# DeltaNet and FNet mixing on one Trainium2 core: another order of the same pieces of work, with fourteen more groups of unread TensorE products

## The chip, the core and the metric

The kernel runs on one core of a Trainium2 chip. Its engines are TensorE (PE in the profile, with PEld for its weight loads), VectorE (DVE), ScalarE (ACT) and GpSimd (POOL); SyncE (SP) issues most of the transfers. The metric is the device time of one execution in microseconds (us), lower is better. The kernel before takes 620.09 us, the median of three runs (620.94, 620.09 and 619.37).

## What is computed

The first half is a delta rule with a state of 48 by 48 for each of 4 batches and 8 heads; the second half mixes the result with two Fourier transforms and sends it through a small network.

```python
k_n = k / (norm(k) + 1e-06)                    # q, k, v: (4, 8, 768, 48)
for t in range(768):
    y[t] = q[t] @ state                        # 48 x 48 for each batch and head
    state += beta[t] * outer(k_n[t], v[t] - k_n[t] @ state)
x = y reshaped to (4, 768, 384)
u = x + real(fft(fft(x, axis=1), axis=2))
un = (u - mean) / sqrt(var + 1e-06)            # over the 384 columns
out = u + relu(un @ w_ch1) @ w_ch2             # 384 x 1536 and 1536 x 384
```

## The kernel before

**Units.** Tokens are handled 128 at a time: 6 tiles for each of 4 batches make 24 units, and a unit holds all 8 heads. Inside a tile the step-by-step rule becomes matrix products: the keys' products with each other give a triangular matrix for each head, which is inverted; queries, keys and values go through it, and only one state step for each half tile (64 tokens) depends on the one before it. For a unit the pieces are: load of k, q and v by SyncE (line 407); "turn", transposes of k and q on TensorE (`tr`, line 353, eight instructions at a time) with copies out of PSUM to SBUF (`copy`: line 359 on ScalarE, line 361 on VectorE); the keys' products (line 350) and their eviction into `gd` on VectorE (line 546); the inverse on VectorE; the queries' products, evicted by line 573; the state chain; the outputs, which free the unit's slot.

**Rounds.** Units 0 and 1 form the first round, 2 to 5 the second, and then come rounds of 4, 4, 4, 3 and 3 units. In the first two rounds the inverse is built of blocks of 16 (`invert16`): one transpose of 32 by 32 blocks into `rr` (line 689), a few row operations on `nr` and `gb` (lines 694 to 729, of which 729 only readies a factor for the values, used by line 605), then fourteen steps of a product and a sum (lines 749 and 755) for each round, a scaling (768), two transposes (774, 778), and a `join` of blocks on TensorE and VectorE (lines 809 and 855). In later rounds `invert` does it in thirty steps on blocks of 32 (lines 936 and 941). Units wait in slots: six of `us` and two in R1; unit 11 also uses columns of a tile that the row views call `R`.

**The second half.** For each batch: folds of the sequence on VectorE (line 1353), two transforms as products on TensorE, layer norm, and the network's two products (tiles `w` and `R`). Its weights are rounded and split before by ScalarE, VectorE and GpSimd (lines 1955 to 1975; line 1972 is GpSimd's). All of TensorE's products go through one helper, line 350; what a product belongs to is told by its tiles.

**The order.** Nothing is issued when it is written down. `P.op` of the class `Plan` (lines 135 to 181) only records a piece: what it issues, and which engines may do it. There are 2882 pieces. The text ORDER (lines 57 to 132) then names them in the order of issue, two signs for each; after the number stands a sign for the engine where a piece has a choice (ScalarE or VectorE for most copies out of PSUM; GpSimd or VectorE for the zeroing of padding, `pads`, line 487), a sign for each of the 8 PSUM banks that it takes, and for a load that SyncE issues the piece after which it may start. `issue` (lines 153 to 179) decodes it. Each engine works through its own instructions in that order, and waits where an input or a buffer isn't ready. Between any two engines only these data waits and the paced loads set the timing.

**Unread products.** A number past the last piece calls `fill` (defined at the end of the kernel's function) with a kind and a bank. Kind 4 is one product of a constant, `pack`, 128x128 by 128x256, into a PSUM bank (line 2178); kind 3 is the same in two products of 64 rows; kind 0 is 18 products of 64x64 (line 2172), issued once at the very start. Nothing reads them. A matmul of 32-bit numbers appears twice in the trace, so that the trace counts two for each product that the program issues.

## Time and profile before

| | before |
|---|---|
| median of three runs | 620.09 us |
| the profiled execution's own time | 620.75 us |
| its span in the trace | 618.9 us |
| mean granted TensorE clock | 0.997 |
| busy: PE, DVE, ACT, POOL | 600.3, 538.4, 272.4, 29.6 us |
| records of the trace: PE, DVE, ACT, POOL | 9742, 1500, 758, 39 |
| DMA, mean over the span | 52 GB/s |

The span is what the trace covers; the execution's own time is 1.85 us longer, and that rest is taken as the same for both kernels. Busy time is the sum of what an engine's instructions took. A row of the timeline has its start and its length in us, the engine, the kernel's line, the output and inputs by the program's names, the shapes and a count; in brackets stands the time for which the engine was idle before it, and what ended that wait. A row of the windows gives, for a stretch of the span, the busy time and count of instructions of each engine, the clock that TensorE was granted, and the DMA engines' busy share.

### The profile page before, as it was taken

What the parts mean: (1) busy time and instruction counts of PE and PEld (TensorE: products, weight loads), DVE (VectorE), ACT (ScalarE), POOL (GpSimd) and SP (SyncE); (2) the same over time, 40 slices, a digit from 0 to 9 for tenths busy, and PEclk for the clock granted to TensorE, in tenths of its full rate; (3) what the DMA queues carried; (4) which work ended last, traced back from release to release, by engine and by line L of the source; (5) the groups of instructions that cost most, each with busy time, mean ns of one, the idle gap of its engine ahead of it and who ended that gap; (6) DMA issues with size and microseconds to landing.
All of it is one profiled execution on the core that took longest, in us unless ns stands there. A gap on an engine that the chain in (4) does not pass through costs nothing.

```text
span 618.9 us, 22537 instructions
## 1 busy us (share of the span) xinstructions
PE 600.3 (97%) x9742; PEld 523.0 (85%) x9742; DVE 538.4 (87%) x1500; ACT 272.4 (44%) x758; POOL 29.6 (5%) x39
## 2 busy tenths in 40 slices
PE   8799899999999999999999999999999999999997
PEld 7578889767777777889888878898899899999997
DVE  5989998999898989999889999998996897878655
ACT  5699667552355354634543323444353304222120
POOL 2003410220000000000000000000000000000000
PEclk9899999999999999999999999999999999999999
DMA  8743554521023222020212121000010000000001
GB/s 162 195 134 103 125 144 120 135 64 35 5 42 70 53 58 66 2 40 14 54 29 66 28 52 28 19 21 15 2 41 4 28 1 2 27 1 26 1 2 51
DMA packets 85440, 31.98 MB, mean 52 GB/s; under 512 B 75996, under 2 KB 80829, under 8 KB 85341
## 3 DMA queue, kind: packets, MB, share of 16 engines
q1 hardware_dynamic: 85149, 30.31, 19.9%
q8 instruction: 76, 1.25, 0.8%
q10 hardware_dynamic: 192, 0.23, 0.1%
q14 instruction: 23, 0.19, 0.1%
HBM read 25.82 MB, written 4.72 MB: 49 GB/s over the span
## 4 chain that ended last, share of the span: by engine, by line
PE 83%; DVE 11%; ACT 2%; issue 2%; DMA 1%; POOL 0%; DVEq 0%; POOLq 0%; ACTq 0%
PE pp L350 79%; PE pp L353 3%; DVE R L1353 2%; ACT us L359 1%; PE pp L2178 1%; DVE pm L1353 1%; DMA us<-in_q_dram 1%; DVE eo L1353 1%; PE pp L2172 1%; DVE rr L689 1%; DVE x L1328 0%; DMA R<-in_moe_w_ch_dram 0%; POOL w L1972 0%; DVE gd L546 0%; DVE tmp L749 0%
## 5 line engine op out<-in xcount | busy, mean ns | idle before, releaser
L350 PE MATMUL pp<-R,w 128*128 128x256 f32 (+1 forms) x832 | 180.6, 366 | 0.0
L350 PEld LDWEIGHTS pp<-R,w 128*128 128x128 f32 x832 | 144.9, 190 | 18.6 <-issue 0.4
L350 PE MATMUL pp<-w,R 128*128 128x384 f32 (+1 forms) x288 | 91.0, 440 | 0.1
L350 PE MATMUL pp<-us 64*64 64x64 f32 (+5 forms) x2704 | 87.6, 233 | 2.2 <-ACT us L359 1.0
L359 ACT ACTIVATE us<-pp 128x512 f32<-128x512 f32 (+4 forms) x149 | 58.6, 402 | 60.4 <-PE pp L350 37.7
L350 PEld LDWEIGHTS pp<-us 64*64 64x64 f32 (+3 forms) x2704 | 74.2, 134 | 8.4 <-ACT us L359 2.8
L350 PEld LDWEIGHTS pp<-w,R 128*128 128x128 f32 x288 | 51.7, 190 | 21.7 <-DVE st L1291 0.2
L936 DVE TENSOR_TENSOR tmp<-rr 128x168 f32<-128x168 f32 (+9 forms) x150 | 50.8, 341 | 2.9
L941 DVE TENSOR_TENSOR rr<-rr,tmp 128x168 f32<-128x168 f32 (+10 forms) x150 | 49.4, 331 | 3.2
L350 PEld LDWEIGHTS pp<-u,us 64*64 64x64 f32 (+1 forms) x1360 | 34.1, 130 | 9.1 <-issue 3.9
L350 PE MATMUL pp<-u,us 64*48 64x48 f32 (+2 forms) x1360 | 40.1, 217 | 1.5 <-DVE mv L361 0.6
L359 ACT ACTIVATE R<-pp 128x384 f32<-128x384 f32 (+9 forms) x60 | 24.4, 426 | 27.3 <-PE pp L353 16.5
L1795 DVE TENSOR_TENSOR us<-us,pp 128x256 f32<-128x256 f32 x64 | 25.9, 417 | 11.8 <-ACT us L359 7.2
L1830 ACT ACTIVATE R<-pp 128x512 f32<-128x512 f32 x23 | 13.7, 596 | 45.0 <-PE pp L350 34.8
L359 ACT ACTIVATE u<-pp 64x192 f32<-64x192 f32 (+1 forms) x60 | 19.6, 326 | 26.4 <-DVE x L1899 13.7
L350 PE MATMUL pp<-R,ws 128*128 128x192 f32 x144 | 28.5, 328 | 0.2 <-issue 0.2
L350 PE MATMUL pp<-us,gd 128*128 128x192 f32 x144 | 27.6, 327 | 0.0
L1607 ACT ACTIVATE R<-pp 128x512 f32<-128x512 f32 x22 | 13.0, 595 | 32.3 <-PE pp L350 32.2
L359 ACT ACTIVATE us<-us,nr 128x48 f32<-128x48 f32 x112 | 26.5, 323 | 0.3 <-DMA us<-in_v_dram 0.2
L350 PE MATMUL pp<-st,us 48*64 48x48 f32 (+1 forms) x1104 | 25.0, 222 | 1.2 <-issue 1.1
L1328 DVE TENSOR_TENSOR x<-x,pp 64x192 f32<-64x192 f32 x66 | 23.2, 351 | 2.1 <-PE pp L350 0.9
L350 PEld LDWEIGHTS pp<-ft,R 97*128 97x128 f32 (+1 forms) x192 | 23.0, 191 | 1.8 <-ACT R L359 0.9
(208 smaller groups left out, 1076.2 us busy)
## 6 DMA issues: line engine op xcount, KB each, us to landing
out_dram<-x SPq DMA_DIRECT2D x11, 384.0 KB
us<-in_k_dram SPq DMA_DIRECT2D x16, 192.0 KB
us<-in_q_dram SPq DMA_DIRECT2D x16, 192.0 KB
us<-in_v_dram SPq DMA_DIRECT2D x16, 192.0 KB
x<-in_moe_w_ch_dram SPq DMA_DIRECT2D x11, 242.0 KB
R<-in_moe_w_ch_dram SPq DMA_DIRECT2D x8, 256.0 KB
ws<-in_moe_w_ch_dram SPq DMA_DIRECT2D x5, 242.0 KB
us<-in_k_dram SPq DMA_DIRECT2D x6, 181.5 KB
```

What stands on the lines that cost most here:

```text
L350: I(nc.tensor.matmul(o, lhsT=lhsT, rhs=rhs, start=start, stop=stop, skip_group_check=True))
L353: I(nc.tensor.matmul(o, lhsT=src, rhs=ident[p0:p0 + n, p0:p0 + n], is_transpose=True, start=start, stop=True, skip_group_check=True))
L359: I(nc.scalar.activation(o, i, ACT.Copy, **({} if scale is None else {"scale": scale})))
L689: vec(1760, lambda e: I(nc.vector.transpose(R, ro.gd(0, 4).rearrange("p (n c) -> p c n", c=32))), [ro.agd(0, 4)], [aR], pr)
L936: I(eng(e).tensor_tensor(T_, R[:, :, j + 1:32, j:j + 1].broadcast_to([128, ns, n, j]), R[:, :, j:j + 1, 0:j].broadcast_to([128, ns, n, j]) ...
L941: I(eng(e).tensor_tensor(R[:, :, j + 1:32, 0:j], R[:, :, j + 1:32, 0:j], T_, op=ALU.add))
L1328: I(nc.vector.tensor_tensor(w, w, v, op=ALU.add))
L1353: I(eng(e).tensor_tensor(o, i0, i1, op=op))
L1607: I(nc.scalar.activation(o, s, ACT.Relu))
L1795: vec(256, lambda e: I(nc.vector.tensor_tensor(o, i0(), i1(), op=ALU.add)), [], [aH] + list(wr), pr - P.ev, use=n)
L1830: I(nc.scalar.activation(o, s, ACT.Relu))
L2172: I(nc.tensor.matmul(pst[0:64, 512 * bank + c:512 * bank + c + 64], lhsT=w[:, 0:64], rhs=w[:, 64:128], start=True, stop=True, skip_group_c ...
```

## The change

Only the 74 lines of ORDER change; every function and every recorded piece stays as it is. The new text differs in all lines, so a line of it tells nothing; the first one reads:

```diff
-AGBAAAEBAPDAWtCBACBAQDAXAODAZAGAbDGAaAaAeABAFDAYABARASAdCAMBAcBAfCAhDEALDA6AGAKDAgBATAiA7AAAUBBMGCAj
+AODARAWAGBAAAPBAEBACBASAJDAMDAIDtCGAHDAZAGAKDAaAaAXABAbBGAcCAdBAeCAAgBAfCAhFGAiAjAUCA7AABMHDBNCAYA6A
```

Decoded, it says this:

- Unread products of kind 4 go from 22 to 34 and of kind 3 from none to 2; the one of kind 0 stays. Ahead of the first state product of unit 0 stand 33 groups' worth in 14 places instead of 20 in 9; near the queries of a later unit, at about 224 us of the trace of before, stand 2 where 1 stood; and the last one, at 306 us, becomes kind 3 and moves ahead of the state step beside it.
- 154 pieces change engine: 79 go from VectorE to ScalarE, 71 from ScalarE to VectorE, 3 from GpSimd to VectorE and 1 from VectorE to GpSimd.
- 260 of TensorE's 520 pieces keep their position in its order, and the mean shift is 1.0 positions (30 at most). VectorE's pieces shift by 7.7 on average, ScalarE's by 4.8, SyncE's by 4.3. The last pieces of TensorE, from 605.8 us of the trace of before, are the same.
- SyncE issues five of the first units' k loads, then one q load and one piece of the weights, and then the sixth k load; before, four k loads, one q load and two k loads.

The first place is TensorE in the first units, from the queries' and keys' products of units 0 and 1 to the first product of the join (`lo`, `w`). Before, rows read so (`us` holds the units' slots, a row of line 353 is a turn):

```order
L350 MATMUL pp<-us 64x64 x32
L2178 MATMUL pp<-pack 128x256 x4
L353 MATMUL pp<-pack,us 128x64 x24
L350 MATMUL pp<-us 64x64 x16
L353 MATMUL pp<-pack,us 128x64 x8
L2178 MATMUL pp<-pack 128x256 x3
L353 MATMUL pp<-pack,us 128x64 x16
L2178 MATMUL pp<-pack 128x256 x4
L350 MATMUL pp<-us 64x64 x16
L350 MATMUL pp<-lo_74,w_65 64x64 x16
```

Now the stretch from the same two keys' pieces reads so:

```order
L350 MATMUL pp<-us 64x64 x32
L2178 MATMUL pp<-pack 128x256
L2178 MATMUL pp<-pack 64x256 x2
L2178 MATMUL pp<-pack 128x256 x6
L353 MATMUL pp<-pack,us 128x64 x8
L2178 MATMUL pp<-pack 128x256 x2
L353 MATMUL pp<-pack,us 128x64 x8
L2178 MATMUL pp<-pack 128x256
L353 MATMUL pp<-pack,us 128x64 x16
L2178 MATMUL pp<-pack 128x256 x4
L353 MATMUL pp<-pack,us 128x64 x8
L2178 MATMUL pp<-pack 128x256
```

Eight groups of unread products stand ahead of the next turn where four stood, and the turns that followed one another now have unread products between them.

The second place is VectorE in the inverse of the first round (`w` holds its matrix, `tmp` the products, `gd` the keys' products of the second round, `nr` the row factors). The piece of the difference, with what is taken out marked - and what is put in marked +:

```order
 L749 TENSOR_TENSOR tmp<-w_66 128x52
 L755 TENSOR_TENSOR w_66<-w_66,tmp 128x2x13x2
+L546 SCALAR_TENSOR_TENSOR gd<-pp,pack,gd 128x8x32
 L749 TENSOR_TENSOR tmp<-w_66 128x72
+L546 SCALAR_TENSOR_TENSOR gd<-pp,pack,gd 128x8x32
 L755 TENSOR_TENSOR w_66<-w_66,tmp 128x2x12x3
+L729 STREAM_TRANSPOSE nr<-nr 128x32
 L749 TENSOR_TENSOR tmp<-w_66 128x88
 L755 TENSOR_TENSOR w_66<-w_66,tmp 128x2x11x4
-L546 SCALAR_TENSOR_TENSOR gd<-pp,pack,gd 128x8x32
+L694 STREAM_TRANSPOSE nr<-bcol 128x32
```

The second round's keys are taken out of PSUM a few steps earlier, and line 729 of the first round, which stood behind the second round's first steps, now stands among the first round's own.

The third place is ScalarE at about 132 us of the trace of before, where the turn of unit 11 (into `R`) and that of a later unit (into `us`) are copied out of PSUM. Before:

```order
L1962 ACTIVATE ws<-ws 128x512
L359 ACTIVATE R_85<-pp 128x512
L359 ACTIVATE us<-pp 128x512 x2
L359 ACTIVATE lo_74<-pp,pack 128x4x32
L1956 ACTIVATE w_66<-x_84 128x512
```

Now:

```order
L1962 ACTIVATE ws<-ws 128x512
L359 ACTIVATE R_85<-pp 128x512 x2
L359 ACTIVATE us<-pp 128x512
L359 ACTIVATE us<-pp 128x2x4x32
L1956 ACTIVATE w_66<-x_84 128x512
```

ScalarE now copies both halves of unit 11's turn, one behind the other; before, VectorE copied the second half (line 361) behind a step of its inverse. One half of the later unit's turn goes to VectorE instead.

More of the change, by code (lines that the diff above doesn't have):

```diff
@@ new lines @@
+BnArBQtGHA9CBqBrtGDC8AQBRBSA-DHBuDIABtGABACBTBvA3AmBBCC2C2BCDEBDAoByBzCuBPGyBRtGABbB2B3tFHtGABEBFCoA
+AB6BUBGtGAtGAB7tGFBVApB+CtAptGHBaB-BgCCBcA1CDtGABdBeCGBfCpGFCHBhtGAGjBVtGBCqCC3ABBICKBiBoCLtGHBHBpC9
+FGC+CCvCDtGHCOBstGECPBZBtCSBwtGECwCCTtGEBxAqC4CC0CGbGbDJCDtGHBYCWCXDDABtGEB0GaBetGHtGHCaCbCxGHDKCB1t
+GEGiBzCrEDGzBpBWGkCeCgCfDECBkDXCiDaCDcFDdDYCChDZCCsDbCtGBDeCDfAB4DgDhDjGmGcC5CDCzAlDitGFDFEFDkHCC3Ge
+DlDoCDmB5B8CyB9DGDnCCABjCBDpBDqHLDgtGGHDC4tGADrCDNCLGdDtCDuCCEC-HGDADsCG0CFC6G7C-HMDvADwDxCDyCCIDLGF
```

141 lines of the change are left out of this document (68 added, 73 removed).

## The prediction

> **What bounds the kernel now.** I read the page's busy shares, then the windows by stage, then TensorE's and VectorE's own rows in the first stage, then TensorE's gaps later on. From the page:
>
> ```profile
> PE 600.3 (97%) x9742; PEld 523.0 (85%) x9742; DVE 538.4 (87%) x1500; ACT 272.4 (44%) x758; POOL 29.6 (5%) x39
> ...
> PEclk9899999999999999999999999999999999999999
> ...
> PE 83%; DVE 11%; ACT 2%; issue 2%; DMA 1%; POOL 0%; DVEq 0%; POOLq 0%; ACTq 0%
> ```
>
> TensorE is busy 97% of the span and makes 83% of the chain that ended last. The clock falls in one slice only, the second. VectorE's 11% of the chain needs a place. The windows, with busy time for PE, PEld, DVE, ACT and POOL in that order, then the clock, the DMA share and GB/s:
>
> ```profile
> 0.00:41.00 41.00, 34.71 (x754) 28.18 (x754) 32.26 (x119) 26.71 (x69) 4.41 (x19) 0.96 0.76 180
> 41.00:75.00 34.00, 30.97 (x1057) 28.20 (x1058) 32.14 (x77) 27.11 (x68) 12.43 (x9) 1.00 0.43 109
> 75.00:600.00 525.00, 519.55 (x7852) 452.51 (x7850) 465.20 (x1283) 218.20 (x621) 12.80 (x11) 1.00 0.16 38
> ```
>
> Up to 41 us TensorE is idle for 41.00 - 34.71 = 6.29 us, up to 75 us for 3.03 more, and in the 525 us behind that for 5.45 in all. So nothing that the change does after 75 us can win more than 5.45, and the start can win more only if TensorE is what sets its end. VectorE's rows for the start say that it isn't alone:
>
> ```profile
> 8.00:20.00 12.00, 11.52 (x34) 1.00 0.82 187
> 20.00:30.00 10.00, 9.90 (x37) 0.83 0.70 178
> 30.00:40.00 10.00, 8.04 (x27) 1.00 0.63 167
> 40.00:63.00 23.00, 22.07 (x60) 1.00 0.37 102
> ```
>
> From 8 to 63 us VectorE works 51.53 of 55 us, on the inverses, nearly without a gap; its one slack is the 1.96 us between 30 and 40. TensorE in the same stretch:
>
> ```profile
> 13.24 0.70 PE L2178 MATMUL pp<-pack 128*128 128x256 f32 x2
> 13.87 0.69 PE L350 MATMUL pp<-us 48*64 48x64 f32 x32
> 14.75 0.69 PE L350 MATMUL pp<-us 48*64 48x64 f32 x32 [0.19 <-ACT us L359]
> 15.38 1.99 PE L2178 MATMUL pp<-pack 128*128 128x256 f32 x8
> 17.30 0.80 PE L353 MATMUL pp<-pack,us 64*128 64x64 f32 x16
> 21.74 0.46 PE L353 MATMUL pp<-pack,us 64*128 64x64 f32 x8 [3.64 <-ACT us L359]
> ...
> 23.34 2.93 PE L2178 MATMUL pp<-pack 128*128 128x256 f32 x6
> 26.20 0.73 PE L353 MATMUL pp<-pack,us 64*128 64x64 f32 x16
> ...
> 33.21 0.69 PE L350 MATMUL pp<-us 48*64 48x64 f32 x32 [0.64 <-ACT us L359]
> ...
> 41.02 0.62 PE L350 MATMUL pp<-u,us 64*64 64x64 f32 x13 [0.28 <-ACT u L359]
> ```
>
> The idle place that the change fills is the 3.64 us ahead of 21.74, where the next turn's PSUM copy is waited for. The row at 41.02 is the first product of unit 0's state chain.
>
> **The unread products.** From the rows: four of them hold TensorE from 15.38 to 17.30, 1.92 us; one from 13.24 to 13.87, 0.63 us. That is 0.43 for each and 0.2 for each group. Three at 23.34 took until 26.20, 2.86 us, where 3 x 0.43 + 0.2 = 1.49 are expected: 1.37 went to a lower clock, which the windows of TensorE (busy time, then the clock) show:
>
> ```profile
> 20.00:25.00 5.00, 3.26 (x52) 0.79 0.44 140
> 25.00:30.00 5.00, 5.00 (x84) 0.87 0.96 217
> ```
>
> At half speed, 0.79 of 5 us means 2 x 0.21 x 5 = 2.1 us and 0.87 means 1.3 us, together 3.4 us right behind the idle 3.64. With eight groups in that idle time the lower clock should not come, so I take the 1.37 back.
>
> [...]
>
> Up to the first product of the join, the new order has 11 more unread products and 4 more places: 11 x 0.43 + 4 x 0.2 = 5.53. Idle time there and the lost clock give 0.19 + 3.64 + 1.37 = 5.20. Up to the state chain there are 13 more in 5 more places: 6.59, against 5.20 + 0.64 = 5.84. So by this sum TensorE comes to unit 0's chain **0.75 later**, even without any new wait. The products themselves win nothing; what they can bring is that turns, evictions and VectorE's steps come in a better order.
>
> **VectorE in the start.** Its rows:
>
> ```profile
> 30.50 0.23 DVE L749 TENSOR_TENSOR tmp<-w 128x88 f32<-128x88 f32 x1
> ...
> 32.15 0.28 DVE L855 SCALAR_TENSOR_TENSOR gd<-pp,pack,gd 128x64 f32<-128x64 f32 x1 [1.43 <-PE pp L350]
> ...
> 33.62 0.21 DVE L755 TENSOR_TENSOR w<-w,tmp 128x88 f32<-128x88 f32 x1
> ...
> 39.26 0.69 DVE L573 TENSOR_TENSOR us<-pp,pack 128x512 f32<-128x512 f32 x1 [0.44 <-DMA R<-in_moe_w_ch_dram]
> ```
>
> Its waits for TensorE and for a bank here are 1.43 + 0.44 = 1.87 us. The new order brings the rows of 30.50 and 33.62, which are the second round's, ahead of the join's first row: 0.23 + 0.21 = 0.44 more on the way to the join, but work done that stood behind the wait before. Three zeroings of padding come to VectorE from GpSimd; they stand ahead of its first copies, where VectorE waits anyhow, so I cost them at nothing. With the join's product at +0.33 and more done by then, I expect that 1.0 of the 1.87 is won and 0.5 given back: **-0.5**. The ends: all of 1.87 won, **-1.9**; or nothing won, TensorE's 0.75 passed on to the chain and the 0.44 as well, **+1.2**. I take the value by the wait of 1.43, since VectorE is what the stage hangs on up to 63 us.
>
> **The place at 132 us.** VectorE copied the second half of unit 11's turn behind a step of its inverse:
>
> ```profile
> 132.12 0.60 ACT L359 ACTIVATE R<-pp 128x512 f32<-128x512 f32 x1 [2.47 <-PE pp L353]
> ...
> 132.66 1.42 DVE L936 TENSOR_TENSOR tmp<-rr 128x238 f32<-128x238 f32 x1
> ...
> 134.01 0.68 DVE L361 COPY R<-pp 128x512 f32<-128x512 f32 x1
> ...
> 134.83 0.89 PE L350 MATMUL pp<-R 48*64 48x128 f32 x24 [1.08 <-ACT lo L359]
> ```
>
> The row of 134.83 names ScalarE's `lo`, but it reads `R`, and the copy of its other half ended at 134.69, so I take that copy as what it waited for. Now ScalarE does it right behind its first half, done by about 132.12 + 2 x 0.6 = 133.3: TensorE's 1.08 should go. The copy that VectorE gets in exchange belongs to a later unit, whose products stand behind. **-1.0** (from -1.08 to 0, if the exchanged copy makes the same wait).
>
> **The places at 195, 199 and 224 us.**
>
> ```profile
> 190.59 0.57 PE L350 MATMUL pp<-u,us 64*64 64x48 f32 x25
> ...
> 195.64 0.46 PE L353 MATMUL pp<-pack,us 64*128 64x64 f32 x8 [0.90 <-DMA us<-in_q_dram]
> ...
> 199.73 0.28 PE L350 MATMUL pp<-u,us 64*48 64x48 f32 x2 [0.37 <-issue]
> ...
> 224.43 0.70 PE L2178 MATMUL pp<-pack 128*128 128x256 f32 x2
> ```
>
> At 195.64 a turn waits 0.90 for a q load, which SyncE may issue only when the outputs that end at about 191.3 have freed the slot. The new order puts the products of these outputs ahead of a piece of 16 products that stood in front of them, some 0.45 us by the row at 190.59: **-0.4** (-0.90 to 0). At 199.73 a product of the network now stands in the gap of 0.37: **-0.3** (-0.37 to 0). At 224.43 a second unread product stands beside the first, 0.43, partly in a gap: **+0.2** (0 to +0.45). The other moves lie beside TensorE's work, which is 99% busy there (519.55 of 525), and I cost them at nothing; without that cover each could cost a fraction of what idle time is left.
>
> **The sum.** -0.5 - 1.0 - 0.4 - 0.3 + 0.2 = -2.0, from the profiled execution's 620.75 to 618.75. The median of the runs, 620.09, lies 0.66 below that execution, so the forecast on the median is **618.1**. The ends: -1.9 - 1.08 - 0.90 - 0.37 = -4.25, 615.8; and +1.2 + 0.45 = +1.65, 621.7. That is the forecast's own range.
>
> **Rivals.**
> A, no gain: VectorE's rows in the start only change places, the lower clock isn't in most executions, and the 1.08 at 134.83 comes back at the exchanged copy. For it speaks that TensorE's sum is 0.75 in the red. The time is that of before, 620.1.
> B, more: turns and second-round keys come early enough that later waits go too. TensorE's 3.03 us of idle time between 41 and 75 us hang on VectorE and ScalarE's evictions; if two thirds go, 2.0 more, it is 616.1. Against it: VectorE is busy 22.07 of 23 us there.
> C, slower: the unread products take away the slack that hid late loads. SyncE's first rows:
>
> ```profile
> 4.34 0.71 SPq L407 DMA_DIRECT2D us<-in_q_dram  x1
> 5.09 1.78 SPq L407 DMA_DIRECT2D us<-in_k_dram  x2
> 6.98 5.36 SPq L407 DMA_DIRECT2D us<-in_q_dram  x3
> ```
>
> Unit 3's k load was issued at 5.09 and now stands behind one more load of each kind, q and weights; at 1.79 us each, as in the third row, its issue comes up to 3.2 us later (8.3). Its turn is put about 2.4 us later in TensorE's order, so 0.8 could be waited for in full; then the idle time with its lost clock comes back elsewhere. Start-up: 0.75 + 0.44 + 0.8 + 1.37 = +3.36. If the places at 195 and 199, which hang on loads and gaps too, bring nothing, -1.0 + 0.2 stay: +2.56, 622.6. By the same sum it is slower by over 0.3% once the row of 41.02 starts 2.66 later, at 43.7 or behind. For it: the DMA engines are busy 0.76 of the first 41 us. Against it: the stage up to 63 us hangs on VectorE, not on that turn.
>
> **How the numbers follow.** About 0.3%, 1.9 us, is what a measurement of this kernel can tell from no change, so the bounds are 618.2 and 621.95. Forecast 0.46, A 0.14, B 0.20, C 0.20. The forecast's point lies just past the bound, so somewhat over half of its chance counts as faster, 0.25, and 0.21 as the same. Faster: 0.25 + 0.20 = 0.45; same: 0.21 + 0.14 = 0.35; slower: C's 0.20. The range from 615.8 holds the forecast, A and most of B (0.74); up to 622.3 it takes in a third of C, 0.80 in all.
>
> **What would show it.** Right: the row behind the eight groups has no wait of over 1 us, the clock stays at 1.00 between 20 and 30 us, VectorE's wait ahead of line 855 is under 1 us, the first product on `R` at about 133 us waits under 0.3 us, and the turn near 195 waits about 0.5. Wrong: unit 0's first state product at 43.7 or later (C), or at 40 or earlier with TensorE's idle time of 41 to 75 us under 1.5 (B); the lower clock still there; a wait of about 1 us near 134 under another name (A).

## The result, and the profile after

The changed kernel takes 624.31 us, the median of 13 executions (621.73 to 631.20), against 620.28 for the kernel before in the same runs (13 executions, 619.28 to 622.11). The ratio is 1.0077, with an interval from 1.0048 to 1.0106: slower by 0.8%, where 618.1 us and a range from 615.8 to 622.3 were forecast.

The 13 times fall into two groups, and the mean granted TensorE clock goes with them: seven at 621.73 to 624.31 with a clock of 0.995 to 1.000, six at 627.48 to 631.20 with 0.983 to 0.989. The kernel before has no such second group in these runs. In the other runs of this study two of its 129 further executions lie there too, 628.60 and 628.95 at 0.980 and 0.984. (Ratios and intervals here and below leave out executions more than 1.5% above the fastest of their kernel, here the one at 631.20.) So there are two questions: why even the profiled execution, at 622.44 us and a clock of 1.000, is slower than the 620.75 of before, and what costs some 6 us more in about half of the executions.

The page of the profiled execution of the changed kernel, busy time first, then the clock in 40 slices, then the chain that ended last:

```profile
PE 604.5 (97%) x9774; PEld 525.9 (85%) x9774; DVE 533.8 (86%) x1494; ACT 273.1 (44%) x766; POOL 32.5 (5%) x37
...
PEclk9999999999999999999999999999999999999999
...
PE 87%; DVE 9%; issue 2%; ACT 2%; DVEq 0%; ACTq 0%
```

The dip in the second slice of the clock is gone, as forecast. TensorE is busy 4.2 us longer, and the span grows by only 1.7. The windows by stage of the changed kernel, busy time for PE, PEld, DVE, ACT and POOL, then the clock:

```profile
0.00:41.00 41.00, 39.49 (x782) 31.40 (x782) 33.07 (x124) 26.98 (x69) 3.96 (x17) 1.00 0.68 164
41.00:75.00 34.00, 29.49 (x1028) 27.02 (x1029) 28.82 (x71) 25.16 (x68) 13.26 (x9) 1.00 0.47 119
75.00:600.00 525.00, 518.70 (x7874) 451.59 (x7875) 462.94 (x1276) 219.36 (x628) 15.23 (x12) 1.00 0.16 39
```

TensorE's idle time up to 41 us falls from 6.29 to 1.51; from 41 to 75 it rises from 3.03 to 4.51, and behind that from 5.45 to 6.30. That is -4.78 + 1.48 + 0.85 = -2.45, and with the busy time +4.17 it makes the +1.72 of the span. The start filled up as planned, and paid nothing out. TensorE's own rows in the start of the changed kernel:

```profile
15.80 4.07 PE L2178 MATMUL pp<-pack 128*128 128x256 f32 x18
19.80 0.46 PE L353 MATMUL pp<-pack,us 64*128 64x64 f32 x8
...
41.15 0.68 PE L350 MATMUL pp<-u,us 64*64 64x64 f32 x16 [0.29 <-ACT u L359]
```

and its windows there (busy time, then the clock):

```profile
20.00:25.00 5.00, 5.00 (x50) 1.00 0.63 199
25.00:30.00 5.00, 5.00 (x108) 1.00 0.51 141
```

Behind the eight groups and the one beside them no turn waits, and unit 0's state chain starts at 41.15, 0.13 later than before. One of VectorE's windows in the changed kernel shows that the stage behind goes worse:

```profile
40.00:63.00 23.00, 19.42 (x56) 1.00 0.44 113
```

From 40 to 63 us VectorE has 3.58 us of idle time where it had 0.93.

**Where half of the executions lose 6 us.** Two further executions of the changed kernel were profiled (the experiments after_look1 and after_look2), and both belong to the second group. TensorE's windows of the first of them, busy time, then the clock:

```profile
93.50:97.00 3.50, 2.04 (x17) 1.00 0.08 22
97.00:110.80 13.80, 13.80 (x126) 0.51 0.48 121
```

The same stretch of work in the first profile of the changed kernel, in which it begins 0.4 us earlier:

```profile
96.60:110.40 13.80, 13.80 (x168) 1.00 0.48 123
```

In 13.8 us TensorE does 126 records instead of 168: half the clock from 97.37 to 111.02, four times the 3.41 us that it lasted in the trace of before (22.86 to 26.27), and a span of 627.1 against 620.6, 6.5 us more. Just ahead of it stands a wait. In the first profile of the changed kernel it reads, on TensorE (the first product of the second Fourier transform, `ft`):

```profile
95.44 0.99 PE L350 MATMUL pp<-ft,R 97*128 97x97 f32 x7 [1.47 <-ACT R L359]
```

In the profile of before, the same product:

```profile
92.65 1.55 PE L350 MATMUL pp<-ft,R 97*128 97x97 f32 x12 [0.66 <-ACT R L359]
```

The wait grew by 0.81 us. Both rows name a copy on ScalarE, but in the changed kernel ScalarE's last copy there ends at 94.53 + 0.52 = 95.05:

```profile
94.53 0.52 ACT L359 ACTIVATE R<-R 95x383 f32<-95x383 f32 x1
```

The wait ends 0.39 later, with VectorE. VectorE's rows ahead of it, in the changed kernel:

```profile
91.19 1.65 DVE L592 SCALAR_TENSOR_TENSOR gd<-us,pack,lo 128x128 f32<-128x128 f32 x2
92.76 0.42 DVE L1967 TENSOR_SCALAR w<-w 128x512 int32<-128x512 int32 x1
93.09 0.68 DVE L573 TENSOR_TENSOR us<-pp,pack 128x512 f32<-128x512 f32 x1
93.69 1.05 DVE L592 SCALAR_TENSOR_TENSOR gd<-us,pack,lo 128x128 f32<-128x128 f32 x1
94.66 0.68 DVE L573 TENSOR_TENSOR us<-pp,pack 128x512 f32<-128x512 f32 x1
95.26 0.14 DVE L361 COPY R<-pp 97x1 f32<-97x1 f32 x1
```

and in the kernel before:

```profile
89.97 1.38 DVE L592 SCALAR_TENSOR_TENSOR gd<-us,pack,lo 128x128 f32<-128x128 f32 x1
91.28 1.28 DVE L573 TENSOR_TENSOR us<-pp,pack 128x512 f32<-128x512 f32 x2
```

The two rows of line 573 take the queries' products of units 6 and 7 out of PSUM. ORDER gives the transform's first product a bank that one of these two units' queries hold: bank 2 before (unit 7's), bank 5 after (unit 6's). (The change gives 351 of the some 385 pieces that take PSUM banks other ones, which its description left out.) Before, the second eviction ends at 91.28 + 1.28 = 92.56, only 0.04 behind ScalarE's last copy of the transform's input (91.09 + 1.43 = 92.52), and the product starts at 92.65:

```profile
91.09 1.43 ACT L359 ACTIVATE R<-pp 96x384 f32<-96x384 f32 x3
```

After, each eviction stands behind rows of line 592, the second ends at 94.66 + 0.68 = 95.34, and the product starts at 95.44. The one-column copy of 95.26 ends there too, at 95.40; which of the two counts is for the experiments.

**Where every execution loses 1.7 us.** The transform's product starts 95.44 - 92.65 = 2.79 later. Of this 0.81 is the wait and 0.13 was there at 41 us, so 1.85 were lost between 41 and 92 us. Waits that the profile puts down to "issue", which means to nothing that it shows, make most of them. The longest of the changed kernel:

```profile
44.21 0.51 PE L350 MATMUL pp<-us 64*64 64x64 f32 x18 [1.15 <-issue]
...
69.50 0.28 PE L350 MATMUL pp<-us 64*64 64x64 f32 x4 [0.68 <-issue]
...
211.26 0.25 PE L350 MATMUL pp<-R 64*32 64x32 f32 x4 [1.33 <-issue]
```

and the longest of before:

```profile
64.62 0.62 PE L350 MATMUL pp<-st,us 48*64 48x64 f32 x26 [0.51 <-issue]
...
306.13 0.33 PE L350 MATMUL pp<-st,us 48*64 48x48 f32 x8 [0.56 <-issue]
```

Those of over 0.15 us sum to 2.0 us in five places before and to 4.0 us in six other places after; between 41 and 92 us they are 0.86 before and 2.10 after, 1.24 of the 1.85. What is common to them is found by counting TensorE's instructions, a product and a weight load for each record (9774 of PE and 9774 of PEld on the page). The page's part on queues shows that instructions come by a DMA queue of their own:

```profile
q8 instruction: 76, 1.25, 0.8%
```

1.25 MB in 76 transfers are 16 KB each, and 2 x 9774 instructions make 257 for each of them. Counted by 256 (a block, from here on), the waits agree: in the 20 traces of this study those at one part of the program begin at nearly the same remainder of the instruction's number by 256, whatever the kernel: 181 at 40 to 50 us, 173 to 181 up to 70 us, 159 near 180, 141 to 149 at 195 to 220, 125 to 135 at 300 to 320, 117 to 119 at 455 to 470. All 111 such waits behind 36 us begin within 8 instructions of that number, where chance would put 7 of them; in the two kernels compared, as many transfers have started by the end of each of their 11 waits as whole blocks of 256 lie ahead of it; and every one of the 111 ends 2.2 to 2.9 us after the start of an instruction transfer, which itself takes 0.88 to 1.45 us. So I take it that TensorE waits for its own instructions, which no run shows by itself: the transfer starts mostly some 70 to 200 instructions ahead of the wait, and these were worked off in less than the 2.2 to 2.9 us. In the changed kernel the transfer ahead of the wait of 1.15 started at 41.27 and took 1.35; TensorE stopped at 43.06, 144 instructions on, and started again at 44.21, 2.94 after the transfer's start.

More unread products move every later instruction to another place in its block. That such waits come and go with the order is thus part of the change, but none of the prediction's terms held them.

After the transform 1.1 of the 2.79 us come back: 1.08 and 0.61 at the two places near 134 and 195 us that the forecast named, less 1.90 - 1.17 = 0.73 more of the instruction waits and a new wait of 0.52 at 131.77; the rest, some 0.6, is spread.

### The profile page after: what moved, and what is told of

The parts are those of the page before. It is cut to its first block, busy times and chain, and to the rows that moved or that the text cites. A ratio compares the mean times of both kernels' runs of the same rounds, so it can differ in the third digit from the quotient of the medians.

```text
span 620.6 us, 22620 instructions
## 1 busy us (share of the span) xinstructions
PE 604.5 (97%) x9774; PEld 525.9 (85%) x9774; DVE 533.8 (86%) x1494; ACT 273.1 (44%) x766; POOL 32.5 (5%) x37
## 3 DMA queue, kind: packets, MB, share of 16 engines
q8 instruction: 76, 1.25, 0.8%
## 4 chain that ended last, share of the span: by engine, by line
PE 87%; DVE 9%; issue 2%; ACT 2%; DVEq 0%; ACTq 0%
PE pp L350 80%; PE pp L353 3%; PE pp L2178 3%; DVE R L1353 1%; DVE tmp L936 1%; PE pp L2172 1%; DVE rr L941 1%; DVE pm L1353 1%; DVE w L1975 1%; ACT u L359 1%; ACT us L359 1%; DVE w L1959 1%; DVE eo L1353 1%; DVE gd L592 0%; DVE x L1899 0%
## 5 line engine op out<-in xcount | busy, mean ns | idle before, releaser
L936 DVE TENSOR_TENSOR tmp<-rr 128x108 f32<-128x108 f32 (+11 forms) x150 | 48.9, 327 | 3.0
L941 DVE TENSOR_TENSOR rr<-rr,tmp 128x108 f32<-128x108 f32 (+10 forms) x150 | 49.2, 329 | 2.7
L350 PE MATMUL pp<-u,us 64*64 64x48 f32 (+2 forms) x1360 | 39.6, 216 | 1.4 <-DVE mv L361 0.8
L1830 ACT ACTIVATE R<-pp 128x512 f32<-128x512 f32 x21 | 12.5, 597 | 48.8 <-PE pp L350 39.0
L359 ACT ACTIVATE x<-pp 64x384 f32<-64x384 f32 (+2 forms) x44 | 18.9, 437 | 24.8 <-DVE u L1268 19.4
L350 PE MATMUL pp<-ft,R 97*128 97x97 f32 (+1 forms) x192 | 23.8, 275 | 1.5 <-ACT R L359 1.5
```

What stands on the lines that cost most here:

```text
L350: I(nc.tensor.matmul(o, lhsT=lhsT, rhs=rhs, start=start, stop=stop, skip_group_check=True))
L359: I(nc.scalar.activation(o, i, ACT.Copy, **({} if scale is None else {"scale": scale})))
L936: I(eng(e).tensor_tensor(T_, R[:, :, j + 1:32, j:j + 1].broadcast_to([128, ns, n, j]), R[:, :, j:j + 1, 0:j].broadcast_to([128, ns, n, j]) ...
L941: I(eng(e).tensor_tensor(R[:, :, j + 1:32, 0:j], R[:, :, j + 1:32, 0:j], T_, op=ALU.add))
L1830: I(nc.scalar.activation(o, s, ACT.Relu))
```

## The experiments

The theory at first was that the start makes the loss, by unread products that push the later instruction blocks to other places. The rival was that some moved piece behind the start makes a new wait. Ratios are to the kernel before in the same runs, with a 95% interval.

**The start alone, and the rest alone.** Up to about 190 us the two kernels' orders were cut and joined crosswise; all pieces keep their engines from the half they come from. The first rows that differ on TensorE, of before_to_190 against before (the outputs of unit 7):

```diff
 MATMUL pp<-R_69,w_65 128x256 x6
 MATMUL pp<-u_72,us 48x48 x8
-MATMUL pp<-us 64x48 x16
 MATMUL pp<-u_72,us 64x48 x16
+MATMUL pp<-us 64x48 x16
```

and after_to_190 differs from the changed kernel from the same place on, the other way round; four PSUM banks had to be chosen anew.

> The changed kernel's order up to unit 7's outputs (190 us), the old order behind it. In the changed kernel's trace the first product of the first batch's second transform is 2.6 us late at 93 us, so the theory 'lost in the start' says that this kernel keeps the loss: 623 to 625 us, with a part of its executions at a lower clock as in the changed kernel. The rival 'lost behind 190 us' (the wait of 1.33 us at 210 us and what follows) says 620.5 to 621.5.

> The old order up to 190 us, the changed one behind it. 'Lost in the start' says 619 to 620.5 us: the old start, and the turn near 195 us waits 0.6 less. 'Lost behind 190 us' says 622 to 624.

Measured: after_to_190 at 629.73 us (625.10 to 635.40), ratio 1.0123 (1.0083 to 1.0162); before_to_190 at 620.01 us, ratio 0.9976 (0.9959 to 0.9992). So the loss lies ahead of 190 us, and the order behind it is worth 1.5 us by itself. The two ratios add up to +0.99%, and the change's own +0.77% lies within their intervals, so these runs don't show that one part's price depends on the other. But one trace hints at it: that of after_to_190 has instruction waits of 7.2 us in sum, and half the clock for 3.4 us at 70.1 and for 6.8 us at 462.6, in the old rest, where the trace of before has none.

**Moving the blocks with nothing else.** The very first unread group of 18 products of 64 columns was made 36 of 32, in both kernels, to move all later instructions by 72 (18 more products, four instructions each) without more work:

```diff
-            for i in range(6 * OPEN):
-                c = 64 * (i % 6)
+            for i in range(12 * OPEN):
+                c = 32 * (i % 12)
```

> The changed kernel with the 18 unread products at the very start cut in half each (36 of 32 columns): the same work, 72 more TensorE instructions ahead of everything. Theory 'instruction loading': several gaps of TensorE that no data wait explains (1.15 us at 42.84, 0.68 at 68.6, 1.33 at 209.7) begin 1.3 to 2.5 us behind the start of a transfer of 16 KB of instructions and end 2.2 to 2.9 us behind it, so TensorE outran the loading; with other boundaries these gaps leave their products for others, and the time moves by 1 us or more, either way. Rival 'order alone': the same gaps before the same products, median within 0.7 of 624.3.

> The kernel before with the same 72 extra instructions at the start. 'Instruction loading': the gaps without a data wait at 64.1, 68.4, 199.4 and 305.6 us (0.51, 0.35, 0.37, 0.56) leave these products, others come, and the time moves by 0.5 to 2 us, more likely up. 'Order alone': 620.3 within 0.5, the gaps where they were.

Measured: 637.21 us, ratio 1.0236 (1.0203 to 1.0269), and 633.68 us, ratio 1.0198 (1.0176 to 1.0220). This doesn't tell the theories apart, because the edit isn't without work. Two of TensorE's rows in before_shift72:

```profile
1.10 7.89 PE L2172 MATMUL pp<-pb 128*64 128x32 f32 x72 [1.10 <-POOL pb L487]
...
13.42 2.07 PE L2178 MATMUL pp<-pack 128*128 128x256 f32 x4
```

In the kernel before the 36 records of 64 columns take 4.11 us; 72 of 32 columns take 7.89, so at this place a record costs 0.11 us at either width, and all that follows starts 3.8 us later. What follows is slow for longer too: four records of line 2178 still take 2.07 us at 13.42, where before they took 1.13 at 8.31 (the windows give a clock of 1.00 at both places), and unit 0's state chain starts at 48.14, 7.1 us late. The remainders at which instruction waits begin stayed as they were, which is all that can be used of these two runs.

**The eight groups alone, and small changes of the count.** In the kernel before, the idle 3.64 us took eight unread products (before_eight), or nine tiny ones of 8 columns and one larger (before_plus40), or 35 tiny and one larger (before_plus144); in the changed kernel two of the eight groups became 24 tiny ones (after_plus88). On TensorE, before_eight:

```diff
 MATMUL pp<-pack 128x256 x4
-MATMUL pp<-pack,us 128x64 x24
+MATMUL pp<-pack,us 128x64 x16
+MATMUL pp<-pack 128x256 x8
+MATMUL pp<-pack,us 128x64 x8
```

before_plus40 (before_plus144 with x35 in place of x9):

```diff
-MATMUL pp<-pack,us 128x64 x24
+MATMUL pp<-pack,us 128x64 x16
+MATMUL pp<-pack 64x8 x9
+MATMUL pp<-pack 128x256
+MATMUL pp<-pack,us 128x64 x8
```

after_plus88:

```diff
-MATMUL pp<-pack 128x256 x6
+MATMUL pp<-pack 128x256 x3
+MATMUL pp<-pack 64x8 x24
+MATMUL pp<-pack 128x256
```

> The kernel before with eight of the larger unread products in the 3.64 us ahead of 21.74, and nothing else: the idea of the change alone. They take 8 x 0.43 + 0.2 = 3.64 us. All theories: TensorE has no idle place there and the clock stays at full speed behind it, 1.4 us of TensorE's time. If TensorE set the end of the start, 1.4 faster; if VectorE does, as the prediction had it, within 0.5. 'Instruction loading' adds: 32 more instructions, waiting from 4.2 to 2.7 us, so 0.9965 to 0.999 of the kernel before.

> The same with 9 tiny products and one larger: 40 more instructions. 'Instruction loading': waiting from 4.2 to 2.3 us, so about 2 us faster, 0.996 to 0.998. 'Order alone': no change (0.999 to 1.001).

> The kernel before with 35 such tiny products and one of the larger ones in the 3.64 us in which TensorE waits ahead of 21.74: 144 more instructions, no more time. 'Instruction loading': by the same estimate the waiting goes from 4.2 to 9.2 us, so 5 us slower, 1.006 to 1.012 of the kernel before, more where a long gap brings a stretch at the lower clock. 'Order alone': no change, or a gain up to 1 us as the idle place is filled.

> The changed kernel with two of the unread products of its group of eight replaced by 24 tiny ones (64 by 8 columns), so that TensorE runs about the same work there but 88 more instructions, and every later block of 256 instructions begins 88 instructions earlier in the work. 'Instruction loading': from the traces, a block's transfer starts some 190 instructions ahead of its first one and is usable 2.3 us later; laid over the changed kernel's own rows, that gives 9.5 us of waiting for the boundaries as they are, and 2.2 us with boundaries 88 earlier. So it falls from about 624 to 617 to 619, the gap of 1.15 us behind 42.8 and that of 1.33 at 209.7 go, and no lower clock comes in the middle. 'Order alone': it stays at 623 to 625.

| kernel | median us | ratio | instruction waits behind 36 us in its profile |
|---|---|---|---|
| before_eight | 621.17 | 1.0017 (0.9992 to 1.0043) | 4.6 us (before: 2.0) |
| before_plus40 | 624.22 | 1.0049 (1.0024 to 1.0074) | 3.6 us |
| before_plus144 | 623.32 | 1.0049 (1.0031 to 1.0067) | 3.1 us |
| after_plus88 | 626.66 | 1.0081 (1.0058 to 1.0104) | 4.0 us (changed kernel: 4.0) |

The forecasts of size failed: before_plus40 was to be faster and is slower, after_plus88 was to be the fastest and isn't better than the change. They were worked out from an estimate that a block comes 190 instructions and 2.3 us ahead, which is too coarse. And the tiny products weren't free: a record of 8 columns takes 0.06 to 0.08 us. In before_plus144 they fill more than the 3.64 us:

```profile
18.16 5.89 PE L2176 MATMUL pp<-pack 128*64 128x8 f32 x70
```

Half the clock follows there from 20.30 to 30.54, and the state chain starts at 45.16 instead of 41.02; in before_plus40 it starts at 41.72, in after_plus88 at 43.19 instead of 41.15. So the times of these three can't be put down to instruction waits. What stands is that the sum of the waits moves with the count of instructions ahead of them: 3.1 to 4.6 us in the three kernels made from the one before, against 0.8 to 2.5 in its own trace and four more that keep TensorE's instructions and their order (before_134, before_626, before_801 and before_801b). after_plus88 shows nothing of the kind: the five traces of the changed kernel's order have 3.2 to 5.0. before_eight is the clearest, since it has no tiny products. TensorE's row of unit 0's first state product in it (the lines of this kernel lie 5 further on):

```profile
40.10 0.62 PE L355 MATMUL pp<-u,us 64*64 64x64 f32 x13 [0.28 <-ACT u L364]
```

and its windows:

```profile
20.00:25.00 5.00, 4.94 (x67) 1.00 0.42 130
```

The clock stays at 1.00 there, the chain starts at 40.10 instead of 41.02, and still the kernel isn't faster: the instruction waits, 2.6 us more than in the trace of before, eat up the 0.9. So the eight groups do what the prediction said, and no gain is measured in the end.

**The places at 134 and 195 us.** before_134 is the kernel before with one copy moved: ScalarE copies both halves of unit 11's turn. On ScalarE:

```diff
 ACTIVATE ws<-ws 128x512
-ACTIVATE R_85<-pp 128x512
+ACTIVATE R_85<-pp 128x512 x2
 ACTIVATE us<-pp 128x512 x2
```

before_134_195 also has the rows of unit 7's outputs shown above for before_to_190, and five PSUM banks that came out differently with them.

> The kernel before, with one copy moved: the second half of unit 11's turn (line 361, VectorE, 134.01) goes to ScalarE right behind the first half, as in the changed kernel. TensorE's instructions and their order are the same, so the boundaries of the instruction blocks stay where they were. The prediction's term says the wait of 1.08 us at 133.8 goes: 1.0 faster, ratio 0.9975 to 0.999. Rival: another input of the same product is late by as much and the time stays.

> The same, and unit 7's outputs one piece earlier on TensorE at 190 us. The two pieces have the same number of instructions, so the boundaries stay. The prediction's two terms: 1.0 and 0.4 to 0.6 faster, ratio 0.9965 to 0.9985, the wait for the q load near 195 us down from 0.90 to about 0.3. 'Instruction loading' expects the gaps at 64, 68, 72, 199 and 305 us to stay within 0.3 of what they were.

Measured: before_134 at 619.42 us, ratio 0.9971 (0.9955 to 0.9988). TensorE's products on `R` in it:

```profile
134.00 1.25 PE L350 MATMUL pp<-R 48*64 48x128 f32 x26
```

The wait of 1.08 is gone, and -0.29% is 1.8 us, more than the 1.08 itself. before_134_195 is at 625.74 us, ratio 1.0074 (1.0046 to 1.0101): the q load is no longer waited for, but two other waits stand in one stretch (the other banks are the likely cause, which no run shows). TensorE there:

```profile
191.99 0.67 PE L350 MATMUL pp<-st,us 48*64 48x48 f32 x28 [0.91 <-ACT R L1607]
...
193.38 0.71 PE L353 MATMUL pp<-pack,us 64*128 64x64 f32 x16 [0.72 <-DVE u L1268]
```

and its windows, busy time, then the clock:

```profile
190.00:194.20 4.20, 2.57 (x117) 1.00 0.81 163
194.20:207.90 13.70, 13.70 (x231) 0.50 0.15 28
```

1.63 us of idle time within 4.20 us, and 13.7 us at half the clock behind. This wasn't expected, and it is the same picture as the changed kernel's at 97 us. It made the second theory: what costs most is a wait somewhere in the middle that trips the clock.

**Two more profiles.** The changed kernel as it is.

> The changed kernel again, for a trace of another execution: about half of its 13 executions took 627 to 631 us at a mean clock of 0.983 to 0.989, the others 621.7 to 624.3 at 0.995 to 1.000. 'Instruction loading' expects its gaps at the same instruction numbers as in the first trace (remainder of 256: 181 near 43 and 48, 175 near 69, 145 to 149 near 200 to 211), and where an execution is at a lower clock, that each stretch at half speed follows a window of 3.4 us that holds over 1.1 us of such gaps, not an idle time from data. 'Order alone' expects the same waits for data as in the first trace and the lower clock behind those.

> The same as the run before it, once more: with about even chances in each, three in four that at least one of the two shows the lower clock.

Measured: 629.57 us with a clock of 0.989 and 630.31 us with 0.986. The half clock lies from 97.37 to 111.02 in the first, from 98.51 to 112.16 in the second, behind the wait ahead of the transform; the second has 3.4 us more of it at 43.90, behind an instruction wait of 1.01 us. In the first the row is

```profile
95.81 2.28 PE L350 MATMUL pp<-ft,R 97*128 97x97 f32 x16 [1.46 <-ACT R L359]
```

Its wait of 1.46 us is the 1.47 of the first profile, where the clock stayed whole. So the same wait stands ahead of half the clock in two profiles and of the whole clock in one: alone it doesn't force the lower clock.

**Which of VectorE's rows is late.** First, the one-column copy was suspected. after_626 gives it back to ScalarE, before_626 moves it to VectorE in the kernel before. On VectorE, after_626 against the changed kernel (before_626 has the same row added):

```diff
 L573 TENSOR_TENSOR us<-pp,pack 128x2x4x64
-L361 COPY R_85<-pp 97x1
 L1975 SCALAR_TENSOR_TENSOR w_66<-x_84,w_66 128x512
```

> The changed kernel, with the copy of one column (97x1) ahead of the second transform back on ScalarE and ahead of the copy beside it, as before the change; TensorE's instructions stay. Theory 'one late copy': the wait of 1.47 us at 93.75 falls to about 0.7, no stretch at half speed begins at 97 us, the executions of 627 to 631 us go, and the median falls from 1.0077 of the kernel before to 1.000 to 1.003: what is left is the work of the unread products and the waits for instructions. Rival 'instruction loading alone': those waits bring the half clock, the slow executions stay, ratio 1.006 to 1.009.

> The kernel before, with that copy alone moved to VectorE, behind the instructions that end at 93.15. 'One late copy': the wait at 92.0 grows from 0.66 to about 1.3 us, 0.7 slower in every execution, and in a part of them 13.7 us at half speed follow, 5 to 6 us more; ratio 1.003 to 1.009, with a wide spread. Rival: 0.7 slower at most, no lower clock, ratio 1.000 to 1.0015.

Measured: after_626 at 624.85 us (621.38 to 632.51), ratio 1.0061 (1.0030 to 1.0093), before_626 at 620.86 us, ratio 0.9994 (0.9981 to 1.0008). The theory of the copy falls with after_626: its second group stays (five of 12 executions at 627.92 to 632.51), and so does its wait. before_626 decides nothing, because the moved copy stands behind the transform's products in ORDER there, and they start at 92.61, ahead of the copy's 93.03. TensorE and VectorE in after_626:

```profile
93.93 2.00 PE L350 MATMUL pp<-ft,R 97*128 97x97 f32 x16 [1.45 <-ACT R L359]
```

```profile
93.15 0.68 DVE L573 TENSOR_TENSOR us<-pp,pack 128x512 f32<-128x512 f32 x1
```

The wait is still 1.45, and the product follows the eviction's end at 93.83 by 0.10, as it did in the changed kernel, while ScalarE's last copy ends at 93.55. So the bank is left as the cause.

Then the evictions themselves. after_801 puts both of them ahead of the rows of line 592, at their place in the kernel before. On VectorE, against the changed kernel:

```diff
 L1959 TENSOR_SCALAR w_66<-w_66 128x512
+L573 TENSOR_TENSOR us<-pp,pack 128x2x4x64 x2
 L592 SCALAR_TENSOR_TENSOR gd<-us,pack,lo_75 128x4x32
 L592 SCALAR_TENSOR_TENSOR gd<-us,pack,lo_74 128x4x32
 L1967 TENSOR_SCALAR w_66<-w_66 128x512
-L573 TENSOR_TENSOR us<-pp,pack 128x2x4x64
 L592 SCALAR_TENSOR_TENSOR gd<-us,pack,lo_75 128x4x32
-L573 TENSOR_TENSOR us<-pp,pack 128x2x4x64
```

before_801 does the opposite in the kernel before, with unit 6's eviction behind three others, and before_801b with the banks left as they are and the eviction behind two. On VectorE, before_801b:

```diff
-L573 TENSOR_TENSOR us<-pp,pack 128x2x4x64 x2
+L573 TENSOR_TENSOR us<-pp,pack 128x2x4x64
 L1975 SCALAR_TENSOR_TENSOR w_66<-ws,w_66 128x512
+L573 TENSOR_TENSOR us<-pp,pack 128x2x4x64
 L361 COPY R_85<-pp 96x1
```

(before_801 has the second row one place further down, behind the copy, and the transform in another bank.)

> The changed kernel with VectorE's two evictions of line 573 (units 6 and 7) ahead of the instructions of line 592 near 91 us. 'Late eviction': the wait of 1.47 us ahead of the second transform falls to 0.6 or 0.7 (the copies on ScalarE end then), no stretch of 13.7 us at half clock, the executions of 627 to 632 us go; ratio 1.000 to 1.004. If the half clock comes from the waits for instructions, the slow executions stay and the ratio is 1.005 to 1.008.

> The kernel before with one of these evictions put behind two other instructions of VectorE, so that it ends near 93.3. 'Late eviction': the wait at 92.0 grows from 0.66 to about 1.4 us, so 0.7 slower in each execution, and 5 to 6 us more in those whose window of the clock holds the whole wait; ratio 1.002 to 1.009 with executions of 625 us and more. Otherwise 1.001 and no lower clock behind 90 us.

> The kernel before with unit 6's eviction (line 573, 91.28) behind the next two instructions of VectorE, so that it ends near 93.15; the second transform takes the same PSUM banks. 'Late eviction': the wait of 0.66 at 92.0 becomes 1.2 to 1.3 us, 0.6 slower in each execution, and a part of the executions has 13.7 us at half clock behind it, 625 us and more; ratio 1.001 to 1.007. Rival, that the half clock needs something else of the changed kernel: 1.001, no execution over 624, no lower clock behind 90 us.

Measured, after_801: 621.20 us (12 executions, 619.74 to 623.25, clocks of 0.997 to 1.000), ratio 1.0000 (0.9983 to 1.0018). No execution of a second group is left, and nothing of the 0.8%. VectorE and TensorE in it:

```profile
91.29 1.28 DVE L573 TENSOR_TENSOR us<-pp,pack 128x512 f32<-128x512 f32 x2
```

```profile
93.92 0.58 PE L350 MATMUL pp<-ft,R 97*128 97x97 f32 x4
94.66 1.58 PE L350 MATMUL pp<-ft,R 95*128 95x97 f32 x12 [0.16 <-ACT R L359]
```

No wait of over 0.16 us is left there, and the transform begins 1.52 us earlier than in the changed kernel.

before_801 is at 620.90 us, ratio 1.0011 (0.9996 to 1.0027): inconclusive, since the transform's second bank is another one there and its wait was only 0.42. before_801b is at 621.48 us, ratio 1.0057 (1.0018 to 1.0096), and its executions fall into two groups like those of the changed kernel: eight at 620.23 to 621.95 with clocks of 0.993 to 0.997, four at 628.80 to 630.04 with 0.980 to 0.984. TensorE and VectorE there:

```profile
93.39 1.55 PE L350 MATMUL pp<-ft,R 95*128 95x97 f32 x12 [1.09 <-DVE R L361]
```

```profile
92.57 0.68 DVE L573 TENSOR_TENSOR us<-pp,pack 128x512 f32<-128x512 f32 x1
```

Here the first four records start at 91.65 in unit 7's bank, and the others wait for unit 6's, until the eviction ends at 93.25. The row names VectorE's copy (line 361, which ends at 93.31), but that copy stands behind these products in ORDER, so that they can't need it. One eviction, moved behind two others on an engine that isn't the bottleneck, makes 8 us in a third of the executions. (The profiled one is among the eight, so the four are known by their mean clock; where their half clock lies isn't shown.) In both directions the same eviction makes the second group come and go, which is what shows the cause.

**A version that beats both.** The kernel before up to 190 us with the copy of before_134, and the changed kernel's order behind it. Its ScalarE differs from before_to_190's by the row shown for before_134.

> The kernel before up to 190 us with the copy of unit 11's turn on ScalarE, the changed order behind 190 us. Each of the two was faster alone, 0.9971 and 0.9976. If they add, 0.994 to 0.996; if the order behind 190 us was faster only because the wait at 134 us was still ahead of it, or new waits for instructions come, 0.996 to 0.999.

Measured: 618.33 us (617.33 to 619.95), ratio 0.9959 (0.9942 to 0.9977): 0.4% faster than the kernel before, and by the two ratios 1.2% faster than the changed one. What the change had to give was in its rest, and in one copy of its start.

## Why the prediction was wrong

**The start (-0.5; from -1.9 to +1.2).** The bounds held at 41 us: the eight groups have no wait behind them, the lower clock between 20 and 30 us is gone, and unit 0's chain starts 0.13 later, where TensorE's sum alone gave 0.75 and the forecast 0.5 earlier. VectorE's wait ahead of line 855 is shorter, though not under 1 us:

```profile
32.44 0.48 DVE L855 SCALAR_TENSOR_TENSOR rr<-pp,pack,rr 128x64 f32<-128x64 f32 x2 [1.19 <-ACT w L1956]
...
50.18 0.47 DVE L855 SCALAR_TENSOR_TENSOR rr<-pp,pack,rr 128x64 f32<-128x64 f32 x2 [2.07 <-ACT u L359]
```

The second row is the second round's join. The same row of before stands 1.37 earlier and waits for nothing:

```profile
48.81 0.48 DVE L855 SCALAR_TENSOR_TENSOR rr<-pp,pack,rr 128x64 f32<-128x64 f32 x2
```

The join takes TensorE's products of `lo` and `w`, and these stand behind two instruction waits in the changed kernel:

```profile
48.22 0.80 PE L350 MATMUL pp<-lo,w 64*64 64x64 f32 x20 [0.27 <-issue]
```

With the 1.15 of 44.21 that is 1.42, about the 1.37 by which the join is late (argued from the rows; no run takes these two waits away alone). So what VectorE won at 32 us is given back at 50. The term's bounds hold at the chain's start and not at the stage's end, because they ended at 41 us and the stage doesn't.

**Taking the 1.37 back.** Right for this place. Rival A's doubt, that the lower clock isn't in most executions, didn't come true: the mean clock of the kernel before is 0.997 at most in 128 of the 129 executions whose clock is on record, so the dip stands in practically each of them. The prediction asked what it is worth to remove one trip of the clock, and didn't ask what a new one would cost elsewhere. A short wait was enough for one: half the clock stands behind 1.46 us of idle time (after_look1, busy 2.04 of 3.50), and behind two waits of 0.91 and 0.72 (before_134_195).

**134 us (-1.0) and 195 us (-0.4).** Right: the wait on `R` is gone, alone worth 0.29% in before_134, and the turn near 195 waits 0.29 instead of 0.90. On TensorE in the changed kernel:

```profile
131.77 0.55 PE L353 MATMUL pp<-pack,pm 128*128 128x128 f32 x3 [0.52 <-DVE pm L1539]
...
194.24 0.71 PE L353 MATMUL pp<-pack,us 64*128 64x64 f32 x16 [0.29 <-ACT u L359]
```

The first row is a new wait just ahead of the turn, which takes half of the 1.08 back; rival A expected such a one at its full length.

**199 us (-0.3) and 224 us (+0.2).** The gap at 199 is gone, but the reading failed: it was a wait for instructions, which no product fills. One of 1.33 us now stands at 211.26. The second unread product at 224 shows no loss.

**The step that failed** is "The other moves lie beside TensorE's work, which is 99% busy there (519.55 of 525), and I cost them at nothing; without that cover each could cost a fraction of what idle time is left." VectorE's pieces move by 7.7 positions on average, and the order of line 573 behind line 592 is one of these moves. It lies beside TensorE's work only as long as no product needs the bank that the eviction empties. One does, and before the change that eviction ended only 0.09 ahead of it (92.56 and 92.65), behind a wait of 0.66. The wait grows by 0.81 us in the profiled execution, and some 6 us of half clock come with it in about half of the executions, not a fraction of the idle time. The instruction waits, 1.24 us more between 41 and 92 us, stand in no term either. A busy share of 99% says how much can be won there. It says nothing about how much can be lost.

**The rivals.** A and B didn't come, B's 616.1 least of all. C had the right sign, and lost clock does come back elsewhere as it said, but not by its mechanism: unit 0's first state product stands at 41.15, not at 43.7 or later, and no load is waited for in the start. Its 622.6 is near the first group's times by chance.

**What stays open.** Why the same wait lowers the clock in six of 13 executions and not in the other seven. Idle time alone doesn't decide. In each trace all changes of the clock lie whole multiples of 3.413 us apart, so the window that held the wait can be laid out, at full clock in the first profile and ahead of half clock in after_look1:

```profile
92.37:95.78 3.41, 1.95 (x13) 1.00 0.17 50
```

```profile
93.95:97.37 3.42, 1.96 (x17) 1.00 0.02 3
```

Both hold the whole wait and are busy for the same time, so that neither decides (the expectation of before_801 took it that holding the whole wait does); they differ in where the wait falls, and so in what fills the rest: mostly products of the first transform (`tab`) in the first, mostly the smaller ones of the second (`ft`) in the other. An estimate of the array's work takes rows times columns that a product uses, times the columns that pass, in units of 128 x 128: some 144 for a record of `tab`, 73.5 for one of `ft`. That makes 1368 in the first profile's window and 1512 in after_626's, which kept the clock, and 1156 and 1086 in those of after_look1 and after_look2, which lost it. Over all 20 traces, of the windows at full clock from 7 to 600 us, half clock follows 14 of 15 under 1060, 9 of 30 up to 1313, and 1 of 3380 above. In the three profiles of the changed kernel the changes stand at other places (0.21, 1.80 and 2.94 us as the rest by 3.413), so what they keep to doesn't begin with the kernel. Windows of 3.41 us with little work in one of them fit the records; no run was made to test it, and between 1060 and 1313 something else decides. Open too is why the half clock lasts one window at some places (3.4 us at 43.90) and four at others (13.7 us at 97 and at 194), and the size of each instruction wait: that they begin at nearly the same place of a block is shown, and how long each becomes after a move couldn't be forecast.

## What to carry to other kernels

When an order is changed, look up for each PSUM bank that the critical engine takes who empties it last, and on which engine, also on engines that are far from busy enough to bound the kernel: a moved eviction is a moved release. Price a new wait of the size seen here (1.1 to 1.5 us) in TensorE's middle also by what the lower clock behind it can take (6.5 us here), not by its own length alone, and measure several executions with their clocks, since one profile can show the good case alone. A place that is filled with unread work moves every later instruction in its block, so the filling has to be tried, not summed.

## What the runs showed of the hardware

- In the traces of this study half clock comes, behind 36 us, after windows of 3.41 us with 1.1 to 1.6 us of idle time (1.46 of 3.42 in after_look1), in some executions and not in others (1.46 of 3.41 in the first profile of the changed kernel, which kept the clock); it lasted 3.4, 6.8, 13.7 or 17.1 us, and 13.7 us cost 6.5 us of span (627.1 against 620.6).
- It can come with no idle time at all: in before_plus144 TensorE is busy for all of 16.89 to 20.30, in good part with products of 8 columns, and half the clock follows for 10.2 us.
- Instructions came in 76 transfers of 16 KB, 257 of TensorE's for each. In stretches of short products (behind the wait of 1.15, 18 records in 0.51 us) TensorE stands idle until 2.2 to 2.9 us after the start of one, up to 1.33 us at once in the two kernels compared and 2.0 and 4.0 us in all; over all traces of this study the sum behind 36 us runs from 0.8 us (before_626) to 7.2 us (after_to_190). Half clock can stand behind such a wait as well: in after_626 3.4 us of it follow the one of 1.33 us at 209.74.
- The releaser that a row names can be a copy that was done earlier, when the wait is for a bank: ScalarE's `R` was named, and VectorE's eviction by line 573 ended the wait, 0.10 us ahead of the product.
- At the very start of the kernel a record of 32 columns took as long as one of 64: 7.89 us for 72 and 4.11 us for 36.
